# Banded attention and a gated MLP on one core: where the block transposes stand in TensorE's stream, and when the output additions run

## The chip, the cores and the metric

The kernel runs on one core of one Trainium2 chip. The metric is the device time of one execution in microseconds (us), as the median of several runs. The engines are TensorE (PE, with its weight loads shown as PEld), VectorE (DVE), ScalarE (ACT), GpSimd (POOL) and SyncE (SP, which issues the DMAs). Each works through its own queue in the order in which the program lists its instructions, and engines wait for one another through semaphores.

## The reference

Eight sequences of 576 positions, eight heads of 64. Half the heads attend to the last 32 positions, the other half to every fourth of the last 128. The attention output goes through an RMS norm and a gated MLP.

```python
scores = scale * np.matmul(q, k.transpose(0, 1, 3, 2))
mask_plain = (rel >= 0) & (rel < window)                                   # window 32
mask_dil = (rel >= 0) & (rel < window * dilation) & (rel % dilation == 0)  # dilation 4
...
attn = np.exp(scores)
attn = attn / (np.sum(attn, axis=-1, keepdims=True) + 1e-09)
return np.matmul(attn, v).astype(np.float32)
...
xn = x / rms * rms_g                       # x: 4608 tokens x 512
g = xn @ w_gate                            # 512 x 1536
silu = g * (1.0 / (1.0 + np.exp(-g)))
val = xn @ w_val
return (silu * val @ w_out).astype(np.float32)
```

## The kernel before

**Units and ticks.** The 4608 tokens are cut into 16 units of 288 (half a sequence). For a unit u, attention produces x, transposed (512 features on partitions in four chunks of 128, 288 tokens free), and the MLP consumes it. The MLP runs over NJ = 12 slices of the hidden size. Each slice is three *ticks*: a gate group (`gate`), a val group (`val`) and the projection of the slice before (`proj`). A tick is 12 large matmuls of 128x128 by 288, since every product is made of three fp32r matmuls (high by high, high by low, low by high; L637, L638, L639 in `three`). Behind the group of a tick `attend` puts the attention work that the plan has for that tick; it belongs to the next unit.

**Blocks.** The attention of a unit is 14 *blocks*: for each of the four chunks (two heads each) three blocks of 96 queries (chunks 0 and 1, plain window) or four of 72 (chunks 2 and 3, dilated). A block goes through these steps:
- scores (`scored`, L499): one matmul per head into a PSUM tile "s"
- maxima (`scores_max`): DVE adds the mask (L370) and finds the row maxima (L375); then ACT exponentials (`scores_exp`, L386), DVE sums and reciprocals (`scores_norm`, L395 and L396), and POOL's scaling (L402)
- transposes (`transposed`, L474): two fp32 transposes on PE, one per head, into a free part of the PSUM tile that the tick's gate or val group wrote, or into a tile of its own on a projection tick
- copies of the transposed block (`untranspose`): ACT makes the high part `pt` (L457), DVE the low part (L459)
- outputs (`output`): two matmuls, L487 with both parts and L488, into a PSUM tile "o", of which there is one
- `take`: ACT copies one part of "o" out (L422); `add`: DVE adds the other part to it (L432), two instructions each

Beside this, for each pair of heads, queries and keys are split into high and low parts (`split`): ACT copies, POOL makes the low part of the keys (L344), DVE that of the queries (L353). Of the MLP, ACT does tanh (L676), DVE the silu part (L681) and the product (L694), ACT and POOL the high and low part of the product (L705, L706).

**The order.** `plan` gives each block a tick for its scores (`q_at`), its transposes (`t_at`) and its outputs (`o_at`), relative to a base of the unit. For units 3 to 15 scores come every second tick from -9 to 17, transposes 5 ticks and outputs 8 ticks behind them. So scores and outputs share a tick, with an even one between that has transposes alone. Work of the other engines is queued by `later(dt, rank, fn)`: it is issued dt ticks on, ahead of that tick's group, in the order of ranks. The ranks that matter here, in the tick of issue: sums of `scores_norm` -1, tanh and product 0, `untranspose` 0.2, `take` and the product's parts 0.5, `scores_max` 0.7, silu part 0.8, queries' low part 0.9, exponentials 2, `add` 4. Positions of a relative tick modulo three tell the group: 0 gate, 1 val, 2 projection. Units below NEX = 3 have blocks in plain fp32 and no additions, and units 1 and 2 have lists of their own (`SCORES`).

Of the kernel before, what the change touches and what calls it, by code (L numbers as in the profile page):

```python
# [29 lines left out]
NEX = 3  # L30
# [28 lines left out]
def geometry(u, c):  # L59


    half = u % 2
    if c < NC // 2:
        if half:
            return [(QB * i, QB * i, 0, P) for i in range(U // QB)], QB, U + W
        return [(QB * i, max(QB * i - W, 0), 0 if i else W, P if i else QB)
                for i in range(U // QB)], QB, U
    nq = U // DIL
    keys = nq + (W if half else 0)
    return [(nq * r, keys * r, 0 if half else W, keys) for r in range(DIL)], nq, keys * DIL  # L70
# [3 lines left out]
def attn_moe(ctx: ExitStack, tc: tile.TileContext, qk_in, v_in, w_gate, w_val, w_out, rms_g, outT):  # L74
# [41 lines left out]
    def later(dt, rank, fn):  # L116
        put_off.setdefault(now[0] + dt, []).append((rank, fn))
# [168 lines left out]
    def load_v(b):  # L286

        if b is not None and b[0] >= NNAT:
            u, c, i = b
            vt = sb.tile([P, 2, D], F32, tag="vt", name=f"vt_{u}_{c}_{i}", bufs=3)  # L290
            nc.sync.dma_start(out=vt.rearrange("p a d -> p (a d)"), in_=v_in[u, c][:, i * 2 * D:(i + 1) * 2 * D])
            vs[b] = vt

    def further(b, n):

        k = everything.index(b) + n
        return everything[k] if k < len(everything) else None
# [6 lines left out]
    def split_v(b, dt):  # L304
        k = everything.index(b) % 2

        def hi():
            if k not in vparts:
                vparts[k] = [late[0].tile([P, 2, D], F32R, name=f"v{p}_{k}", bufs=1) for p in ("hi", "lo")]
            A.copy(out=vparts[k][0], in_=vs[b])  # L310

        def lo():
            vh, vl = vparts[k]
            G.tensor_tensor(out=vl, in0=vs.pop(b), in1=vh, op=ALU.subtract)  # L314
            load_v(further(b, 3))

        later(dt, 3.3, hi)
        later(dt, 5.1, lo)

    def after(u, h, n):  # L320

        k = u * H + h + n
        return divmod(k, H) if k < NU * H else None
# [82 lines left out]
    def take(u, c, i, o):  # L406

        blocks, nq, _ = geometry(u, c)
        if (u, c) not in xraw:
            xraw[u, c] = sb.tile([P, U], F32, tag="xraw", name=f"xraw_{u}_{c}", bufs=NC)  # L410
        x = xraw[u, c]
        if c < NC // 2:
            to = x[:, QB * i:QB * i + nq]
        else:
            to = x.rearrange("p (j r) -> p r j", r=DIL)[:, i, :]
        copy = V.tensor_copy if i % 2 and u == 0 and c == NC - 1 else A.copy
        if u < NEX:
            for a in range(2):
                copy(out=to[a * D:(a + 1) * D], in_=o[a * D:(a + 1) * D, a * nq:(a + 1) * nq])
        else:  # L420
            for a in range(2):
                A.copy(out=to[a * D:(a + 1) * D], in_=o[a * D:(a + 1) * D, (2 + a) * nq:(3 + a) * nq])  # L422
        if i == len(blocks) - 1:
            later(1, 2.5 if u else 1.9, lambda: square(u, c))

    def add(u, c, i, o):
        _, nq, _ = geometry(u, c)
        x = xraw[u, c]
        to = x[:, QB * i:QB * i + nq] if c < NC // 2 else x.rearrange("p (j r) -> p r j", r=DIL)[:, i, :]
        for a in range(2):  # L430
            rows = slice(a * D, (a + 1) * D)
            V.tensor_tensor(out=to[rows], in0=o[rows, a * nq:(a + 1) * nq], in1=to[rows], op=ALU.add)  # L432
# [18 lines left out]
    def untranspose(b, t_ps):  # L451
        blocks, nq, _ = geometry(*b[:2])
        n = blocks[b[2]][3]
        t_in = t_ps[:n].rearrange("k (a q) -> k a q", a=2)[:, :, :nq]
        exact = b[0] < NEX
        st[b] = pt = sb.tile([P, 2, 2, QB], F32 if exact else F32R, tag="pt", name=f"pt_{b[0]}_{b[1]}_{b[2]}", bufs=2)
        A.copy(out=pt[:n, 0, :, :nq], in_=t_in)  # L457
        if not exact:
            V.tensor_tensor(out=pt[:n, 1, :, :nq], in0=t_in, in1=pt[:n, 0, :, :nq], op=ALU.subtract)  # L459

    def products(q, t, o, t_ps, s_tag="s", o_tag="o"):


        if q:
            s_ps = ps.tile([P, 512], F32, tag=s_tag, name=f"s_{q[0]}_{q[1]}_{q[2]}")
        if o:
            o_ps = ps.tile([P, 512], F32, tag=o_tag, name=f"o_{o[0]}_{o[1]}_{o[2]}")
            pt = st.pop(o)
        if t:
            p, _ = st.pop(t)  # L470
        def transposed(a):
            blocks, nq, _ = geometry(*t[:2])
            n = blocks[t[2]][3]
            PE.transpose(t_ps[:n, a * QB:a * QB + nq], p[:nq, a, :n], ident[:nq, :nq])  # L474

        def output(a):
            blocks, nq, _ = geometry(*o[:2])
            n = blocks[o[2]][3]
            if a:
                return  # L480
            out = o_ps[:, :2 * nq].rearrange("d (a q) -> d a q", a=2)
            if o[0] < NEX:
                PE.matmul(out, vs.pop(o)[:n].rearrange("k a d -> k (a d)"), pt[:n, 0, :, :nq], start=True, stop=True)
                return
            vh, vl = (part[:n].rearrange("k a d -> k (a d)") for part in vparts[everything.index(o) % 2])
            both = o_ps[:, :4 * nq].rearrange("d (t a q) -> d t a q", t=2, a=2)
            PE.matmul(both, vh, pt[:n, :, :, :nq], start=True, stop=False)  # L487
            PE.matmul(out, vl, pt[:n, 0, :, :nq], start=False, stop=True)  # L488

        def scored(a):  # L490
            blocks, nq, _ = geometry(*q[:2])
            qc, kc, _, n = blocks[q[2]]
            sv = s_ps[:QB].rearrange("q (a t k) -> q a t k", a=2, t=2)
            if q[0] < NEX:
                qk = heads[q[0], 2 * q[1] + a]
                PE.matmul(sv[:nq, a, 0, :n], qk[:, qc:qc + nq], qk[:, U + kc:U + kc + n], start=True, stop=True)
                return
            qs, ks = heads[q[0], 2 * q[1] + a]
            PE.matmul(sv[:nq, a, :, :n], qs[:, qc:qc + nq], ks[:, :, kc:kc + n], start=True, stop=True)  # L499

        parts = [(b, fn, a) for b, fn in ((t, transposed), (o, output), (q, scored)) for a in range(2)]
        for b, fn, a in parts:
            if b:
                fn(a)
        if t:
            later(1, 0.2, lambda: untranspose(t, t_ps))
        if o:
            later(1, 0.5, lambda: take(*o, o_ps))
            if o[0] >= NEX:
                later(1, 4, lambda: add(*o, o_ps))  # L510
            if o[0] < NEX:
                later(1, 9, lambda: load_v(further(o, 3)))
            far = further(o, 2)
            if far and far[0] >= NEX:
                split_v(far, 8 if o[0] < NEX else 1)
        if q:
            later(1, 0.7, lambda: scores_max(*q, s_ps))
            later(2, 2, lambda: scores_exp(*q))
            later(3 if q[0] < NNAT else 4, -1, lambda: scores_norm(*q))
            u, c, i = q  # L520
            nxt = after(u, 2 * c, 2)
            nb = len(geometry(u, c)[0])
            if u < NEX:
                if u == NNAT - 1 and c == NC - 1 and i == nb - 1:
                    for h in range(4):
                        later(1, 9, lambda h=h: load(NNAT, h))
                if u >= NNAT and i == nb - 1 and c < NC - 1:
                    for a in range(2):
                        later(1, 9, lambda a=a: load(*after(u, 2 * c + a, 4)))
                if u == NEX - 1 and c == NC - 1 and i == nb - 1:  # L530
                    for a in range(2):
                        later(3 + a, 9, lambda a=a: split(NEX, a, (1, 2, 2, 3), G, V))
            elif nxt and i == 0:
                split(*nxt, (1, 2, 2, 3), G, V)
                split(nxt[0], nxt[1] + 1, (2, 3, 3, 4), G, V)
# [242 lines left out]
    plan(0, 0, range(nb), range(LAG, nb + LAG), range(LAG + OUT, nb + LAG + OUT))  # L778
    for u in range(1, NU):
        q_at = [LAST - (LAST - EARLY) * (nb - 1 - k) // (nb - 1) for k in range(nb)]  # L780
        t_at, o_at = [t + 5 for t in q_at], [t + 8 for t in q_at]
        if u <= NNAT:
            q_at = SCORES[u]
            t_at, o_at = [t + 5 for t in q_at], [t + (7 if u < NNAT else 8) for t in q_at]
        plan(u, ends - 2 + 3 * NJ * (u - 1), q_at, t_at, o_at)
# [20 lines left out]
    for u in range(NU):  # L806
        for j in range(NJ):
            for part in range(0 if u + j else 2, 3):
                t = 3 * (u * NJ + j) + part
# [94 lines left out]
```

## Time and profile before

| | |
|---|---|
| median of 3 runs | 1129.47 us (1128.94 to 1130.58) |
| profiled execution | 1129.25 us, its span 1127.4 us |
| granted TensorE clock | 1.000 |
| PE busy | 1116.9 us, 99% of the span |
| DVE, ACT, POOL busy | 779.8 us (69%), 700.6 us (62%), 602.5 us (53%) |
| chain that ended last | PE 94%, DVE 2%, DMA, issue, POOL and ACT 1% each |

The span is the time from the first to the last instruction in one profiled execution. In a timeline row the columns are start, duration, engine, line, operation, output and inputs, shapes, and how many instructions were merged ("x2"); in brackets the idle time before, with what ended it. A matmul's duration contains its way through the array, and matmuls overlap, so distances between starts tell what one costs. In a grouped row the number behind the bar is the busy time in us, then the mean duration in ns. In a row of the waits stand the waiting engine with tile and line, what released it, the total in us, the number of waits and the longest.

### The profile page before, as it was taken

To read this page: it belongs to the slowest core of one execution; us is meant where nothing else is said; L and a number is where in the kernel's file an instruction comes from. 1 tells how busy PE (TensorE), PEld (TensorE's weight loads), DVE (VectorE), ACT (ScalarE), POOL (GpSimd) and SP (SyncE) were. 2 spreads that over 40 slices of the span, in tenths; PEclk is the share of its full clock that TensorE was granted. 3 is DMA by queue.
4 is the path that set the end of the run, shared out by engine and by line. 5 is a ranking of instruction groups with operands and counts; after the bars stand their busy time and mean duration, and the time that the engine had idled before them with its cause. 6 is when DMAs were issued, how large, how long until landed. Compare 5 with 4: busy or idle time off the path is not lost.

```text
span 1127.4 us, 25853 instructions
## 1 busy us (share of the span) xinstructions
PE 1116.9 (99%) x8385; PEld 1088.4 (97%) x8385; DVE 779.8 (69%) x2837; ACT 700.6 (62%) x2578; POOL 602.5 (53%) x1051
## 2 busy tenths in 40 slices
PE   9999999999999999999999999999999999999998
PEld 7787999999999999999999999999999999999998
DVE  6888768758587675867758587675868767586311
ACT  6795576757667575666757576575756757575311
POOL 8323566646556554655646565564655646475211
PEclk9999999999999999999999999999999999999999
DMA  9566212303122121311212122131312212120000
GB/s 252 172 223 220 71 43 68 100 26 90 40 81 61 31 82 40 93 52 50 85 39 83 41 71 65 34 89 36 96 44 65 76 34 82 41 81 15 10 14 22
DMA packets 61544, 82.19 MB, mean 73 GB/s; under 512 B 7298, under 2 KB 41090, under 8 KB 61410
## 3 DMA queue, kind: packets, MB, share of 16 engines
q1 hardware_dynamic: 61410, 80.54, 23.6%
q8 instruction: 67, 1.10, 0.4%
q14 instruction: 67, 0.55, 0.2%
HBM read 71.08 MB, written 9.44 MB: 71 GB/s over the span
## 4 chain that ended last, share of the span: by engine, by line
PE 94%; DVE 2%; DMA 1%; issue 1%; POOL 1%; ACT 1%; SPq 0%; POOLq 0%; DVEq 0%; ACTq 0%
PE acc L637 9%; PE v L637 9%; PE g L637 9%; PE acc L638 8%; PE acc L639 8%; PE g L638 8%; PE v L638 8%; PE v L639 8%; PE g L639 8%; PE s L499 3%; PE o L487 3%; PE acc L634 2%; PE v L634 2%; PE g L634 2%; PE o L488 1%; PE t L474 1%
## 5 line engine op out<-in xcount | busy, mean ns | idle before, releaser
L706 POOL TENSOR_TENSOR hlo<-th,hhi 128x288 fp32r<-128x288 f32 x180 | 146.0, 811 | 202.3 <-ACT hhi L705 151.9
L639 PE MATMUL acc<-hhi,lo 128*128 128x288 f32 x720 | 212.4, 295 | 0.0
L402 POOL TENSOR_SCALAR t<-t,sum 72x72 f32<-72x72 f32 (+3 forms) x414 | 153.5, 383 | 73.9 <-DVE sum L396 63.8
L639 PE MATMUL g<-xhi,lo 128*128 128x288 f32 x612 | 180.2, 295 | 0.0
L639 PE MATMUL v<-xhi,lo 128*128 128x288 f32 x612 | 180.2, 294 | 0.0
L705 ACT CAST hhi<-th 128x288 fp32r<-128x288 f32 x180 | 78.1, 434 | 153.0 <-DVE th L694 150.4
L386 ACT ACTIVATE t<-t,sum 96x128 f32<-96x128 f32 (+3 forms) x448 | 166.0, 375 | 10.8 <-DVE sum L375 10.3
L676 ACT ACTIVATE th<-g 128x288 f32<-128x288 f32 x180 | 73.8, 410 | 107.2 <-PE g L639 89.2
L314 POOL TENSOR_TENSOR vlo<-vt,vhi 128x128 fp32r<-128x128 f32 x182 | 86.2, 473 | 101.3 <-ACT vhi L310 87.4
L639 PEld LDWEIGHTS acc<-hhi,lo 128*128 128x128 f32 x720 | 135.4, 188 | 0.0
L432 DVE TENSOR_TENSOR xraw<-o,xraw 64x72 f32<-64x72 f32 (+1 forms) x364 | 99.2, 273 | 50.5 <-ACT xraw L422 44.6
L681 DVE SCALAR_TENSOR_TENSOR th<-th,g 128x288 f32<-128x288 f32 x180 | 80.5, 447 | 71.3 <-ACT th L676 67.5
L639 PEld LDWEIGHTS g<-xhi,lo 128*128 128x128 f32 x612 | 115.2, 188 | 0.0
L639 PEld LDWEIGHTS v<-xhi,lo 128*128 128x128 f32 x612 | 115.1, 188 | 0.0
L637 PE MATMUL g<-xhi,hi_g 128*128 128x288 f32 x357 | 111.4, 312 | 0.8 <-DVE th L694 0.8
L637 PE MATMUL acc<-hhi,hi_o 128*128 128x288 f32 x360 | 110.7, 307 | 0.0
L694 DVE TENSOR_TENSOR th<-th,v 128x288 f32<-128x288 f32 x180 | 81.5, 453 | 38.0 <-PE v L639 30.0
L638 PE MATMUL acc<-hlo,hi_o 128*128 128x288 f32 x360 | 106.4, 296 | 0.0
L422 ACT COPY xraw<-o 64x72 f32<-64x72 f32 (+1 forms) x364 | 94.1, 258 | 11.7 <-PE o L488 9.6
L370 DVE TENSOR_TENSOR t<-s,mask 96x256 f32<-96x256 f32 (+3 forms) x182 | 66.8, 367 | 47.6 <-PE s L499 42.9
L344 POOL TENSOR_TENSOR ks<-qk,ks 128x288 fp32r<-128x288 f32 (+2 forms) x104 | 99.6, 973 | 0.0
L638 PE MATMUL g<-xlo,hi_g 128*128 128x288 f32 x322 | 94.9, 295 | 0.0
(189 smaller groups left out, 3566.5 us busy)
## 6 DMA issues: line engine op xcount, KB each, us to landing
qk<-in_qk_dram SPq DMA_DIRECT2D x60, 288.0 KB, 2.9
vt<-in_v_dram SPq DMA_DIRECT2D x196, 64.0 KB, 1.8
qk<-in_qk_dram SPq DMA_DIRECT2D x30, 352.0 KB, 3.0
out_dram<-ot SPq DMA_DIRECT2D x64, 144.0 KB, 1.9
qk<-in_qk_dram SPq DMA_DIRECT2D x30, 304.0 KB, 2.8
raw<-in_w_gate_dram SPq DMA_DIRECT2D x12, 512.0 KB, 4.5
raw<-in_w_val_dram SPq DMA_DIRECT2D x12, 512.0 KB, 5.3
raw<-in_w_out_dram SPq DMA_DIRECT2D x12, 512.0 KB, 4.5
```

Of the source, the lines that this page charges most:

```text
L314: G.tensor_tensor(out=vl, in0=vs.pop(b), in1=vh, op=ALU.subtract)
L344: ek.tensor_tensor(out=ks[:, 1, :nkt], in0=kr, in1=ks[:, 0, :nkt], op=ALU.subtract)
L386: A.activation(out=t[:nq, a, :n], in_=t[:nq, a, :n], func=AF.Exp, scale=-1.0, bias=sm[:nq, a, 0:1], accum_out=sm[:nq, a, 1:2] if u or i % ...
L402: (V if u == 0 and (c, i) > (NC - 1, 0) else G).tensor_scalar(out=t[:nq, a, :n], in0=t[:nq, a, :n], scalar1=sm[:nq, a, 3:4], scalar2=1.0, ...
L422: A.copy(out=to[a * D:(a + 1) * D], in_=o[a * D:(a + 1) * D, (2 + a) * nq:(3 + a) * nq])
L432: V.tensor_tensor(out=to[rows], in0=o[rows, a * nq:(a + 1) * nq], in1=to[rows], op=ALU.add)
L637: PE.matmul(out, wh[:, cc, :], xh, start=start, stop=False)
L638: PE.matmul(out, wh[:, cc, :], xl, start=False, stop=False)
L639: PE.matmul(out, wl[:, cc, :], xh, start=False, stop=stop)
L681: V.scalar_tensor_tensor(out=t, in0=t, scalar=1.0, in1=g, op0=ALU.add, op1=ALU.mult)
L694: V.tensor_tensor(out=t, in0=t, in1=v_ps[:, :U], op=ALU.mult)
L706: G.tensor_tensor(out=lo, in0=t, in1=hi, op=ALU.subtract)
```

## The change

For units 3 to 15 the transposes move from 5 to 6 ticks behind their block's scores, so that they fall on the tick that has outputs and scores of other blocks; outputs stay at 8. Within such a tick the order becomes outputs, transposes, scores in place of transposes, outputs, scores. Ticks without transposes, or with transposes of units 0 to 2, are issued in the old order. The additions move from the tick behind the outputs (rank 4, near its end) to the tick after that (rank 0.3, behind sums and product).

```diff
-        parts = [(b, fn, a) for b, fn in ((t, transposed), (o, output), (q, scored)) for a in range(2)]
+        order = ((o, output), (t, transposed), (q, scored))
+        if not t or t[0] < NEX:
+            order = ((t, transposed), (o, output), (q, scored))
+        parts = [(b, fn, a) for b, fn in order for a in range(2)]
...
             if o[0] >= NEX:
-                later(1, 4, lambda: add(*o, o_ps))
+                later(2, 0.3, lambda: add(*o, o_ps))
...
         q_at = [LAST - (LAST - EARLY) * (nb - 1 - k) // (nb - 1) for k in range(nb)]
-        t_at, o_at = [t + 5 for t in q_at], [t + 8 for t in q_at]
+        t_at, o_at = [t + 6 for t in q_at], [t + 8 for t in q_at]
```

## The prediction

> **What bounds the kernel now.** I read the page's busy shares first, then the waits, then TensorE's timeline by the start of each instruction, then the timelines of VectorE (DVE) and ScalarE (ACT) around one block.
>
> ```profile
> PE 1116.9 (99%) x8385; PEld 1088.4 (97%) x8385; DVE 779.8 (69%) x2837; ACT 700.6 (62%) x2578; POOL 602.5 (53%) x1051
> PE o L487 <- DVE xraw L432: 0.3, 1, 0.3
> ACT pt L457 <- DVE th L694: 91.5, 65, 1.9
> ```
>
> TensorE is busy all through and almost never waits: the wait view has 0.3 us for the output matmul L487 behind an addition. So time can be won only by a denser PE stream, and any new wait of PE is paid in full. DVE at 69% has no bound of its own, but its queue is in order. The third row: ACT's copy of the transposed block waits until DVE's product has read the same PSUM tile.
>
> The price of a transpose pair, standing alone between two groups (96 wide, then 72 wide):
>
> ```profile
> 605.44 0.33 PE L474 MATMUL v<-ident,t 96*128 96x96 f32 x2
> 605.55 0.38 PE L637 MATMUL acc<-hhi,hi_o 128*128 128x288 f32 x1
> 605.77 0.29 PE L638 MATMUL acc<-hlo,hi_o 128*128 128x288 f32 x1
> ...
> 706.11 0.29 PE L474 MATMUL v<-ident,t 72*72 72x72 f32 x2
> ...
> 706.42 0.29 PE L638 MATMUL acc<-hlo,hi_g 128*128 128x288 f32 x1
> ```
>
> ```profile
> L474 PE MATMUL g<-ident,t 96*128 96x96 f32 x62 | 10.2, 246 | 0.0
> L474 PE MATMUL v<-ident,t 72*104 72x72 f32 x42 | 6.1, 225 | 0.0
> L637 PEld LDWEIGHTS acc<-hhi,hi_o 128*128 128x128 f32 x360 | 67.7, 188 | 0.0
> L499 PEld LDWEIGHTS s<-ks,qs 128*72 128x72 f32 x208 | 22.9, 142 | 0.0
> ```
>
> ```profile
> 614.90 0.34 PE L487 MATMUL o<-pt,vhi 128*128 128x384 f32 x1
> 615.07 0.25 PE L488 MATMUL o<-pt,vlo 128*128 128x192 f32 x1
> 615.16 0.36 PE L499 MATMUL s<-ks,qs 128*72 128x208 f32 x2
> 615.35 0.31 PE L637 MATMUL v<-xhi,hi_g 128*128 128x288 f32 x1
> ...
> 618.72 0.29 PE L487 MATMUL o<-pt,vhi 104*128 104x288 f32 x1
> ...
> 708.00 0.23 PE L488 MATMUL o<-pt,vlo 72*128 72x144 f32 x1
> 708.07 0.34 PE L637 MATMUL g<-xhi,hi_g 128*128 128x288 f32 x1
> 708.25 0.29 PE L638 MATMUL g<-xlo,hi_g 128*128 128x288 f32 x1
> ```
>
> From 615.35 to 618.72 lie 24 large matmuls and one transpose pair. With the pair at 0.18 (next sentence) a large matmul takes (3.37 - 0.18) / 24 = 0.133 us. From the first transpose to the second large matmul pass 0.33 us (96 wide) or 0.31 (72); less one large matmul, a pair costs 0.197 or 0.177. Its inside: two merged transposes take 0.33, one 0.246, so the second starts 0.084 after the first; at 72, 0.29 - 0.225 = 0.065. That leaves 0.112 from the second transpose to the large matmul, for either width. The short output matmul L488 shows the same: 708.00 to 708.25 is 0.25, less 0.133, so 0.117 in rounded rows. So a short matmul ahead of a large one costs 0.11, whatever it streams; I read that as the 128 weight columns of the large one, loaded while nothing long covers them. The score matmul's load is shorter, 142 against 188 ns: 0.112 - 0.046 = 0.066.
>
> **The change, part by part.** It concerns units 3 to 15, 13 units of 14 blocks; units 0 to 2 keep the order, the ticks of the transposes and have no additions.
>
> *Transposes between outputs and scores.* Now the pair stands alone in the tick between two block ticks; then it follows the output matmuls and precedes the scores of other blocks, or the next group where no scores come. The step into the pair is covered in both places (the short output matmul streams 0.07 to 0.09 anyway, and had the score weights to cover). The step out of it falls from 0.112 to the transposes' own pace, 0.084 or 0.065, since 0.066 of score weights fit in. Saved: 0.028, say 0.026 at 96, and 0.045 at 72. Where no scores follow, the 0.112 behind L488 goes and L488's own 0.066 stays: 0.045 too. Bounds: nothing, if the scores' load after a transpose is as dear as a large one's; 0.112 per block, if the step out vanished.
>
> ```profile
> L432 DVE TENSOR_TENSOR xraw<-o,xraw 64x72 f32<-64x72 f32 x208 | 59.6, 286 | 46.4 <-ACT xraw L422 43.2
> L432 DVE TENSOR_TENSOR xraw<-o,xraw 64x96 f32<-64x96 f32 x156 | 39.6, 254 | 4.1 <-ACT xraw L422 1.4
> ```
>
> Two additions a block make 104 blocks of 72 and 78 of 96: 104 x 0.045 + 78 x 0.026 = 6.7 us saved. The Trainium skill ("TensorE: Matmul & The Clock Gate", section on LDWEIGHTS) has a weight load take its columns divided by 1.2 ns, so 107 ns for 128 columns and 60 for 72; by it the saving would be 22 and 42 ns a block, 6.1 us. The trace agrees: 188 - 142 = 46 ns for 56 columns.
>
> *One tick more between scores and transposes, one less between transposes and outputs.* GpSimd's normalisation gets a tick more, and nothing waited for it. ACT's copy and DVE's low part (L457, L459) lose one of three ticks. No DMA is issued by a moved step, and SP's and GpSimd's queues keep their order. But the copy and the low part (rank 0.2) now stand in the tick after a block tick, ahead of the maxima of its scores (rank 0.7), and DVE cannot start the maxima before them.
>
> *Additions one tick later, rank 0.3.* They leave the end of that tick and go behind the next tick's sums (rank -1) and product (rank 0). There is one PSUM tile "o": the next outputs wait for the addition, and outputs now lead the block's PE work, so transposes and scores queue behind that wait. Before, they had slack:
>
> ```profile
> 615.62 0.37 DVE L370 TENSOR_TENSOR t<-s,mask 72x208 f32<-72x208 f32 x1 [0.84 <-PE s L499]
> 616.41 0.45 DVE L681 SCALAR_TENSOR_TENSOR th<-th,g 128x288 f32<-128x288 f32 x1
> 616.77 0.52 DVE L432 TENSOR_TENSOR xraw<-o,xraw 64x96 f32<-64x96 f32 x2
> 617.32 0.15 DVE L395 TENSOR_REDUCE sum<-sum 72x2 f32<-72x4 f32 x1
> 617.71 0.45 DVE L694 TENSOR_TENSOR th<-th,v 128x288 f32<-128x288 f32 x1
> ```
>
> ```profile
> 620.73 0.29 PE L474 MATMUL g<-ident,t 72*104 72x72 f32 x2
> 621.11 0.41 ACT L676 ACTIVATE th<-g 128x288 f32<-128x288 f32 x1
> 621.42 0.27 ACT L457 CAST pt<-g 104x144 fp32r<-104x144 f32 x1
> 621.72 0.31 DVE L459 TENSOR_TENSOR pt<-g,pt 104x144 fp32r<-104x144 f32 x1 [0.37 <-ACT pt L457]
> 621.95 0.44 DVE L681 SCALAR_TENSOR_TENSOR th<-th,g 128x288 f32<-128x288 f32 x1
> 682.60 0.30 DVE L370 TENSOR_TENSOR t<-s,mask 72x144 f32<-72x144 f32 x1 [0.83 <-PE s L499]
> 683.25 0.45 DVE L681 SCALAR_TENSOR_TENSOR th<-th,g 128x288 f32<-128x288 f32 x1
> ```
>
> ```profile
> 730.69 0.41 DVE L370 TENSOR_TENSOR t<-s,mask 96x256 f32<-96x256 f32 x1
> 731.67 1.40 DVE L353 TENSOR_TENSOR qs<-qk,qs 64x288 fp32r<-64x288 f32 x1
> 733.10 0.52 DVE L432 TENSOR_TENSOR xraw<-o,xraw 64x96 f32<-64x96 f32 x2
> ...
> 733.77 0.41 PE L487 MATMUL o<-pt,vhi 128*128 128x384 f32 x1
> 734.02 0.25 PE L488 MATMUL o<-pt,vlo 128*128 128x192 f32 x1
> 690.79 1.01 DVE L353 TENSOR_TENSOR qs<-qk,qs 64x288 fp32r<-64x288 f32 x1
> ```
>
> I work in time after the first large matmul behind a block's scores; the next outputs are due 24 x 0.133 = 3.2 us later. The pair stands 0.26 before that zero (scores start 0.19 before it, 615.16 to 615.35, and a 72-wide transpose 0.065 earlier) and ends at -0.03.
>
> *Gate ticks* (a block tick behind a gate group: relative ticks 3, 9 and 15 of a unit, taking positions modulo three from the code). ACT's tanh reads the transposes' PSUM tile, so it starts 0.09 behind their end (621.02 to 621.11), copy 0.31 and low part 0.61 after tanh's start: the low part at 0.67, the maxima 0.23 later (621.72 to 621.95) at 0.90. Maxima 0.79 (615.62 to 616.41): the silu part at 1.69. Then 0.36 (616.41 to 616.77), sums and reciprocal 0.39 (617.32 to 617.71), the product 0.38 (0.45 long, overlapped like the silu part): the addition at 2.82, ending at 3.34 (0.52), or 3.40 at 72 (two of 0.286). PE starts 0.15 after that (733.62 to 733.77) and its first output matmul holds 0.25 instead of 0.17 (615.07 - 614.90): 0.22 in all, so 3.56 to 3.62 against 3.2. With 0.05 for a wider low part at tick 3, the wait is about 0.4 in the 7 odd units. In the 6 even units the maxima of 72 keys take 0.65 (682.60 to 683.25): 0.26. Together 21 x 0.40 + 18 x 0.26 = 13 us.
>
> *Val and projection ticks.* Behind a val group the product comes first (0.45), then copy and low part: maxima at about 1.07, no silu or second product before the addition; it ends at 2.8 to 2.9, in time by 0.1 to 0.2. Behind a projection the copy goes at once, and the addition ends near 2.4.
>
> *Where a query's low part (L353) stands between maxima and addition* (ticks -1, 5 and 13): beside GpSimd's key parts it takes 1.40, 0.84 to 1.03 or, undisturbed, 0.46. Tick 13 (val): 1.07 + 0.79 + 1.0 + 0.39 + 0.59 + 0.22 = 4.06, 0.85 late; with 0.84, 0.7. Tick -1: 0.45 late in even units; 1.0 in odd ones (1.40), where the trace already has about 0.25 (o1 at 733.77). Tick 5: 0.34 in even units, none in odd. That is 7 x 1.45 + 6 x 1.6 = 20 us; with 0.46 throughout it is 3. GpSimd's work shifts too, so I cannot place the overlap; I take 15, nearer to the rows shown.
>
> **The sum.** The profiled execution took 1129.25 us (span 1127.4 and 1.85 around it; the median, 1129.47, is the same within 0.02%). 1129.25 - 6.7 + 13 + 15 = 1150.5 us, 1.9% more.
>
> **The rivals.**
> A. *The denser stream alone; the additions land in time.* One mechanism: the chain from the transposes to the addition is 0.4 us shorter than I add up, as when DVE's overlaps are larger or the maxima go earlier. The additions decide from 3.2 us on: under 2.98 at their end costs nothing. For it: DVE is idle 31% of the time, and val and projection ticks have room. Against it: each interval in the chain is a measured row, and the order is fixed by ranks. Time: 1129.25 - 6.7 = 1122.5, or 1121 with the old waits of tick -1 gone (7 x 0.25).
> B. *Only the gate ticks wait, the query parts run undisturbed.* For it: odd units had 0.46 at tick 5. Against: overlap elsewhere. 1129.25 - 6.7 + 13 + 3 = 1138.5.
> C. *The pair does not become cheaper*: the scores' weights after an f32 transpose load as slowly as a large matmul's, and with the additions in time nothing changes: 1129, 1130. Against it: the load's length follows its columns.
> D. *The waits are larger*: with the query parts at their full length and 0.2 more at each of 39 gate ticks from ACT's queue (copy behind late exponentials), 1129.25 - 6.7 + 13 + 20 + 8 = 1163.5.
>
> **How the numbers follow.** A difference under about 0.2% (2.3 us) is what a measurement here can't tell from none. Forecast 0.37, B 0.2, D 0.1: slower, 0.67. A 0.25: faster. C 0.08: same. The likeliest case is the forecast, 1150.5, with 1141 (q parts between B and mine) to 1157 (all of the 20) as its own range. The range over all goes from A's 1121 to 1159, leaving out D's upper part and the lowest tail.
>
> **What would show it.** In the changed profile the gap between a transpose pair's end and the scores should be 0.065 to 0.084 us instead of 0.112 to a large matmul; PE's waits should show L487 released by DVE's L432 some 50 to 80 times, 15 to 30 us in total, at gate ticks and at ticks -1, 5, 13. DVE's low part should come ahead of the maxima, and DVE idle before it behind ACT's copy. If L487 has no such waits and the time is near 1122, the chain was shorter than summed (A); if PE has the waits and the pair still costs 0.18, C's half is right. Most likely to make me wrong: the overlap of L353 with GpSimd, and a DVE interval of 0.2 us that overlaps in the new order.

## The result and the profile after

The changed kernel takes 1160.29 us (median of 5 runs, 1158.71 to 1160.75) against 1129.0 us before: a ratio of 1.027, 95% interval 1.0259 to 1.0281. The span of the profiled execution went from 1127.4 to 1158.5 us. Predicted were 1150.5 us and a range from 1121 to 1159: slower, as forecast, but by 31.3 us instead of 21, and just outside the range.

The page of the changed kernel: busy times, and the chain that ended last (before, PE had 94% of it).

```profile
PE 1129.6 (98%) x8385; PEld 1084.9 (94%) x8385; DVE 743.9 (64%) x2837; ACT 701.2 (61%) x2578; POOL 598.5 (52%) x1051
PE 77%; DVE 11%; ACT 7%; issue 2%; DMA 2%; POOL 1%; POOLq 0%; SPq 0%; ACTq 0%; DVEq 0%
```

DVE does less than before (743.9 us busy against 779.8) and yet stands in the chain. The waits of the changed kernel say why (waiting engine, tile and line; releaser; total us, count, longest us; behind line 501 the lines of the changed kernel are 3 higher):

```profile
DVE pt L459 <- ACT pt L457: 182.2, 175, 3.0
PE o L487 <- DVE xraw L432: 12.0, 26, 0.6
PE v L640 <- DVE pt L459: 5.9, 12, 0.8
PEld v L640 <- DVE pt L459: 11.4, 23, 1.0
PEld o L487 <- ACT t L386: 17.3, 26, 0.8
PEld o L487 <- ACT hhi L708: 4.6, 21, 0.4
```

The row of L459 in the kernel before:

```profile
DVE pt L459 <- ACT pt L457: 39.6, 97, 0.8
```

PE has two new waits. The first was forecast: the output matmul L487 behind the addition. The second was not: the val group L640 behind DVE's low part L459, which reads the PSUM tile that this group takes next (the expectations call its place a bank). And DVE stands idle 182 us, not 40, for ACT's copy of the transposed block.

The view counts only idle time and splits a wait between PE and its weight loads (PEld). The last two rows are no other cause: the records have all 63 weight loads of outputs before which PEld stood idle for over 0.15 us start 0.115 to 0.117 us after the end of an addition (26 + 21 named ACT, 16 without a name). So I also take, from the records of the 182 blocks, the distance from the start of each L487 (and of the L488 behind it) to the instruction ahead, less its undisturbed pace, and the same for large matmuls within groups: **outputs wait 29.5 us (2.9 before), groups 12.7 (none before)**. The starts say what each waits for: 72 of the 182 output matmuls wait, and each starts 0.145 to 0.148 us after the end of an addition; 26 val groups wait, and each starts 0.055 us after the end of a low part. With the forecast 6.7 for the denser stream, 1127.4 - 6.7 + 26.6 + 12.7 = 1160.0 against the measured span of 1158.5. In all kernels below that have the new order this account comes out 1.5 to 2.4 us above the span.

One block behind a projection (tick -1 of an odd unit) shows both. ACT's timeline of the changed kernel:

```profile
609.08 0.43 ACT L708 CAST hhi<-th 128x288 fp32r<-128x288 f32 x1 [1.50 <-DVE th L697]
609.42 0.43 ACT L620 CAST spare<-xraw 128x288 fp32r<-128x288 f32 x1
609.76 0.40 ACT L386 ACTIVATE t<-t,sum 96x128 f32<-96x128 f32 x1
...
610.54 0.52 ACT L339 CAST ks<-qk 128x416 fp32r<-128x416 f32 x1
610.97 0.43 ACT L348 CAST qs<-qk 128x288 fp32r<-128x288 f32 x1
611.30 0.30 ACT L457 CAST pt<-t 128x192 fp32r<-128x192 f32 x1
```

DVE's:

```profile
608.62 0.43 DVE L697 TENSOR_TENSOR th<-th,v 128x288 f32<-128x288 f32 x1
609.88 0.91 DVE L621 TENSOR_TENSOR xlo<-xraw,spare 128x288 fp32r<-128x288 f32 x1 [0.83 <-ACT spare L620]
611.64 0.36 DVE L459 TENSOR_TENSOR pt<-t,pt 128x192 fp32r<-128x192 f32 x1 [0.85 <-ACT pt L457]
611.91 0.41 DVE L370 TENSOR_TENSOR t<-s,mask 96x256 f32<-96x256 f32 x1
...
612.90 0.60 DVE L353 TENSOR_TENSOR qs<-qk,qs 64x288 fp32r<-64x288 f32 x1
...
613.80 0.50 DVE L432 TENSOR_TENSOR xraw<-o,xraw 64x96 f32<-64x96 f32 x2
```

PE's:

```profile
609.27 0.34 PE L487 MATMUL o<-pt,vhi 128*128 128x384 f32 x1
...
609.94 0.29 PE L640 MATMUL g<-xhi,hi_g 128*128 128x288 f32 x1
...
611.39 0.29 PE L642 MATMUL g<-spare,lo 128*128 128x288 f32 x1
612.05 0.40 PE L640 MATMUL v<-xhi,hi_g 128*128 128x288 f32 x1 [0.37 <-DVE pt L459]
...
614.46 0.41 PE L487 MATMUL o<-pt,vhi 128*128 128x384 f32 x1 [0.55 <-DVE xraw L432]
```

The block's outputs start at 609.27, and its transposes and scores are through by 610.1. But ACT comes to the copy only at 611.30: the product's high part, another cast, exponentials and copies of keys and queries stand ahead in its queue. DVE meanwhile has the maxima to do, whose scores are there, and stands in order for the copy. The low part ends at 612.00; the val group starts at 612.05 instead of 611.52. Maxima, query part, sums and addition take 2.30 us from there (612.00 to 614.30), but PE has only the twelve matmuls of that group, 1.6 us, before the next outputs: these wait too, 0.79 us on average by the account.

### The profile page after: what moved, and what is told of

Read it like the earlier page. It is cut to its first block, busy times and chain, and to the rows that moved or that the text cites. A ratio compares the mean times of both kernels' runs of the same rounds, so it can differ in the third digit from the quotient of the medians.

```text
span 1158.5 us, 25708 instructions
## 1 busy us (share of the span) xinstructions
PE 1129.6 (98%) x8385; PEld 1084.9 (94%) x8385; DVE 743.9 (64%) x2837; ACT 701.2 (61%) x2578; POOL 598.5 (52%) x1051
## 4 chain that ended last, share of the span: by engine, by line
PE 77%; DVE 11%; ACT 7%; issue 2%; DMA 2%; POOL 1%; POOLq 0%; SPq 0%; ACTq 0%; DVEq 0%
PE acc L640 7%; PE g L640 7%; PE acc L641 7%; PE g L641 7%; PE g L642 7%; PE acc L642 7%; PE v L640 6%; PE v L642 6%; PE v L641 6%; PE o L487 3%; PE s L499 2%; DVE t L375 2%; PE acc L637 2%; PE v L637 2%; ACT t L386 2%
## 5 line engine op out<-in xcount | busy, mean ns | idle before, releaser
L402 POOL TENSOR_SCALAR t<-t,sum 72x72 f32<-72x72 f32 (+3 forms) x414 | 151.0, 377 | 67.3 <-DVE sum L396 59.8
L642 PE MATMUL g<-xhi,lo 128*128 128x288 f32 x612 | 180.2, 294 | 0.0
L432 DVE TENSOR_TENSOR xraw<-o,xraw 64x72 f32<-64x72 f32 (+1 forms) x364 | 97.2, 267 | 20.5 <-ACT xraw L422 18.0
L640 PE MATMUL acc<-hhi,hi_o 128*128 128x288 f32 x360 | 108.9, 302 | 0.0
L640 PE MATMUL g<-xhi,hi_g 128*128 128x288 f32 x357 | 107.6, 301 | 0.8 <-DVE th L697 0.8
L344 POOL TENSOR_TENSOR ks<-qk,ks 128x288 fp32r<-128x288 f32 (+2 forms) x104 | 97.5, 952 | 0.0
L375 DVE CUSTOM_DVE_ANT_0 t<-s,t 96x128 f32<-96x128 f32 (+3 forms) x364 | 81.5, 259 | 6.3
```

Source lines behind the costliest of these rows:

```text
L344: ek.tensor_tensor(out=ks[:, 1, :nkt], in0=kr, in1=ks[:, 0, :nkt], op=ALU.subtract)
L375: V.tensor_tensor_reduce(out=t[:nq, a, :n], in0=sv[:nq, a, 0, :n], in1=plus, op0=ALU.add, op1=ALU.min, scale=-(0.5 if u == NNAT else 1.0) ...
L402: (V if u == 0 and (c, i) > (NC - 1, 0) else G).tensor_scalar(out=t[:nq, a, :n], in0=t[:nq, a, :n], scalar1=sm[:nq, a, 3:4], scalar2=1.0, ...
L640: PE.matmul(out, wh[:, cc, :], xh, start=start, stop=False)
L642: PE.matmul(out, wl[:, cc, :], xh, start=False, stop=stop)
```

## The experiments

Two explanations were tried first. **The additions' new place** costs the waits (then undoing it, or doing it alone, tells). Or **DVE's idleness in order**: the low part, at rank 0.2 ahead of ready work, makes DVE wait for ACT, and each delay comes back through product, high part and copy. The letters in the quoted expectations name the theories as they stood at each time; they are not the prediction's rivals. Intervals are 95%, of the ratio to the kernel before as it was timed beside each. The waits are those of one profiled execution, whose time can lie 1 to 2 us from the median.

| kernel | median us | ratio | outputs wait us | groups wait us | DVE waits for the copy us |
|---|---|---|---|---|---|
| before | 1129.0 | 1 | 2.9 | 0 | 39.6 |
| after | 1160.29 | 1.0259 to 1.0281 | 29.5 | 12.7 | 182.2 |
| 1 additions back | 1168.22 | 1.0329 to 1.036 | 11.9 | 39.1 | 186.6 |
| 2 additions alone | 1166.01 | 1.031 to 1.0341 | 39.4 | 0 | 94.2 |
| 3 additions back, old order | 1165.11 | 1.0301 to 1.0332 | 18.7 | 32.8 | 180.2 |
| 4 low part late | 1136.32 | 1.0045 to 1.0079 | 4.9 | 13.6 | 49.7 |
| 5 low part by group | 1133.64 | 1.0029 to 1.0059 | 5.6 | 12.6 | 69.1 |
| 7 low part late, additions back | 1144.84 | 1.0126 to 1.016 | 0.6 | 26.5 | 55.8 |
| 8 low part late, old order | 1139.21 | 1.0076 to 1.0106 | 14.1 | 14.3 | 49.3 |
| 11 additions alone, ahead | 1131.72 | 1.001 to 1.0028 | 5.2 | 0 | 30.4 |
| 14 ACT copies moved | 1151.58 | 1.019 to 1.0218 | 32.8 | 0.8 | 161.2 |
| 13 = 5 with ACT copies moved | 1132.33 | 1.0019 to 1.0043 | 8.1 | 5.5 | 63.3 |
| 15 = 13, low part early behind projections | 1139.83 | 1.0089 to 1.0116 | 20.5 | 1.8 | 120.1 |
| 17 = 13 with additions ahead of sums | 1130.86 | 1.001 to 1.0028 | 2.4 | 11.1 | 59.0 |

(In 3 and 8 the outputs' column holds a constant share of the old order, where L488 follows L487 later. The outputs that start right behind an addition's end wait 7.0 us there in 3 and 0.8 in 8.)

**1. Additions back** in their old place, the rest of the change as it is; **3** the same with the old order in the tick.

```diff
-                later(2, 0.3, lambda: add(*o, o_ps))
+                later(1, 4, lambda: add(*o, o_ps))
```

> The changed kernel with the additions put back to the tick behind the outputs (rank 4). Theory A (the late additions hold up the outputs): behind gate ticks the waits of the output matmuls go (8 us of 29.5), at ticks 1 and 7 they shrink by the 0.39 us of the sums, to about 8 us in all; the waits of val groups (12.7 us) stay, since they hang on the copy of the transposed block; about 1139 us. Rival B (the waits come from the transposes' new tick alone, the place of the additions does not matter): 1157 to 1160 us.

> As e1_add_back, but within a tick transposes come first again, then outputs, then scores. Theory A: the pair is followed by 128 weight columns again, so the 6.7 us of the denser stream are lost, while ACT and DVE start on the transposed block 0.26 us earlier, which takes up to 0.26 us from each of some 50 waits: between e1_add_back and 7 us above it. If the saving does not come from the order, it is equal to e1_add_back or below.

Both main figures missed. The outputs' waits fell by 17.6 us as they should, but the groups' rose by 26.4, and the whole got slower: the additions now stand ahead of the product, so the product's high part on ACT and the copy behind it come later (read from the order, not tried alone). The new place is not what makes the changed kernel slow; in this layout it is the better one. With the old order (3) the time fell by 3.1 us instead of rising, which is the expectation's other branch, that the order saves nothing. The account says otherwise: from 1 to 3 the outputs' waits fall by 4.9 us (11.9 to 7.0) and the groups' by 6.3, and of these 11.2 us the looser stream takes back 6.7. That leaves 4.5, and the two profiled spans differ by 4.4.

**2. The additions' new place alone**, on the kernel before; **11** the same at rank 0.1, ahead of the low part.

```diff
-                later(1, 4, lambda: add(*o, o_ps))
+                later(2, 0.3, lambda: add(*o, o_ps))   # 2;  11: later(2, 0.1, ...)
```

> The kernel before with nothing but the additions moved one tick on (rank 0.3). Theory A: with the maxima at the head of their tick the additions end at about 3.0 us of the 3.4 that they have, so only the odd units' first outputs wait longer, by 0.39 us: 1130 to 1135 us. Rival C (the additions' move alone makes most of the loss): 1145 us or more.

> The kernel before with the additions one tick on, but at rank 0.1: behind sums and product, ahead of the transposed block's low part (as e2_add_only, which has them at 0.3, behind it). Theory E (in e2_add_only the additions waited behind the low part, which waits for ACT's copy of a transpose issued only one tick earlier): nearly all of its 37 us go, 1130 to 1135 us. If sums and product alone make the additions late: 1150 us or more.

The wait of DVE for the copy in kernel 2:

```profile
DVE pt L459 <- ACT pt L457: 94.2, 144, 1.4
```

Its timelines in one tick, by engine:

```profile
622.56 0.33 PE L474 MATMUL v<-ident,t 96*128 96x96 f32 x2
...
623.42 0.32 ACT L457 CAST pt<-v 128x192 fp32r<-128x192 f32 x1 [1.13 <-DVE th L694]
...
623.77 0.36 DVE L459 TENSOR_TENSOR pt<-v,pt 128x192 fp32r<-128x192 f32 x1 [0.39 <-ACT pt L457]
624.04 0.51 DVE L432 TENSOR_TENSOR xraw<-o,xraw 64x96 f32<-64x96 f32 x2
...
624.71 0.42 PE L487 MATMUL o<-pt,vhi 128*128 128x384 f32 x1 [0.20 <-DVE xraw L432]
```

In the old layout copy and low part run in the tick in which the additions now fall. The additions need nothing fresh, but stand behind the low part, which does: 37 us. At rank 0.1 instead of 0.3, 34 of them are gone. The first was a miss, the second within its figure.

**4. The low part behind the maxima** (rank 0.75), else the changed kernel; **5** the same, but the low part early (0.25) behind val groups.

```diff
-        if not exact:
-            V.tensor_tensor(out=pt[:n, 1, :, :nq], in0=t_in, in1=pt[:n, 0, :, :nq], op=ALU.subtract)
...
+            if t[0] >= NEX:
+                later(1, 0.75, lambda: low_part(t, t_ps))
```

(`low_part` is the line taken out, as a function of its own.)

> The changed kernel with DVE's low part of the transposed block behind the maxima (rank 0.75 in place of 0.2). Theory A: DVE's chain starts 0.4 us earlier, so the waits of outputs behind gate ticks go (8 us); but the low part frees the PSUM tile 0.8 us later, so the groups that reuse its bank wait longer, by 20 to 30 us in all: 1170 to 1185 us. Rival B, and any theory in which DVE's order within the tick plays no part: 1160 us.

> e4_low_late with the low part back ahead of the maxima (rank 0.25) at val ticks alone, where the tile's bank is wanted 1.6 us later by the next gate group. Theory D (DVE idles in its order for ACT's copy; the low part must only be early where the bank is wanted soon): the waits of groups behind blocks at ticks 1, 7 and 13 go (5 us), the rest stays: 1130 to 1133 us. If the low part ahead of the maxima is dear at val ticks too: 1138 us or more.

Kernel 4's waits:

```profile
DVE pt L464 <- ACT pt L457: 49.7, 43, 2.1
DVE t L370 <- PE s L504: 102.5, 91, 2.0
```

One instruction a block moved behind the maxima of the same tick (L370 and two of L375), and 24.0 of the 31.3 us are gone. Both figures of the expectation missed, 1170 to 1185 us and 1160. DVE's wait for the copy falls from 182 to 50 us; what it waits for instead is scores that PE hasn't made yet, which costs PE nothing. This shows the main cause: not how much DVE has to do, but that it stood in order behind a copy that wasn't ready. The Trainium skill ("PSUM — Partial Sum Buffer", section on engine and sequencer instructions) calls the queues of ScalarE, VectorE and GpSimd strict FIFO; the 0.85 us ahead of L459 at 611.64, with ready maxima behind it, agree. Kernel 5 takes 2.7 us more off, close to its figure, though the two intervals overlap.

**7 and 8**: kernel 4 with the additions back at (1, 4), and kernel 4 with the old order.

> e4_low_late with the additions back in the tick behind the outputs (rank 4). Theory D: the waits of outputs (4.9 us) go, but the product and with it ACT's exponentials and the next copy come 0.5 us later, which adds 5 to 15 us of waits of val and gate groups: 1136 to 1147 us. Theory A as first written (late additions alone make the loss): 1131 us.

> e4_low_late with transposes ahead of outputs within a tick. The denser stream's 6.7 us are lost and some waits shrink as ACT starts 0.26 us earlier: 3 to 7 us above e4_low_late, so 1139 to 1143 us. If the order saves nothing: 1136 us or less.

Both as expected. 7: the new place of the additions is worth 8.5 us here, through the groups' waits (26.5 against 13.6). 8: the order outputs, transposes, scores is worth 2.9 us net.

**6, 9, 10 and 12: the query parts.** 6 and 9 are kernel 5 with the ticks of the splits changed, to get the query's low part away from maxima and additions; 10 is 9 with the low part late behind gate groups alone; 12 is the splits of 9 on the kernel before.

```diff
-                split(*nxt, (1, 2, 2, 3), G, V)
-                split(nxt[0], nxt[1] + 1, (2, 3, 3, 4), G, V)
+                split(*nxt, (1, 2, 1, 2), G, V)               # 6: (1, 2, 1, 3)
+                split(nxt[0], nxt[1] + 1, (3, 4, 3, 4), G, V) # 6: (3, 4, 3, 5)
```

> e5_val_early with ACT's copies of the next heads' keys and queries moved out of the odd ticks, where they stand ahead of the copy of the transposed block, into even ones, behind it. Theory D: the late copy behind ticks -1 and 5 comes early, and the waits of val groups there (8 us in e4_low_late) go: 1122 to 1126 us, under the kernel before. If those waits come from something else than ACT's order: as e5_val_early.

> e5_val_early with ACT's copies for the next heads in even ticks (as in e6_splits), but DVE's low parts of the queries in odd ticks, where they stand behind the additions. Theory D: the copies' gain of e6_splits (7 us fewer waits of val groups) stays and its waits of outputs behind ticks 1, 7 and 15 (14 us of 23) go: 1122 to 1127 us, below the kernel before. If the order of these splits does not carry the waits: 1133 us.

> e9_splits_odd with the low part ahead of the maxima at projection ticks too, so that only gate ticks have it behind. Theory D: ACT's copy is early there now, so DVE hardly idles for it and the val group two ticks later gets its bank 0.8 us sooner: 1 to 4 us below e9_splits_odd. If DVE's idling for the copy still counts: above it.

> The kernel before with the splits of e9_splits_odd and nothing else. Its stream has 2.9 us of waits of outputs to win, so 1126 to 1130 us; what e9_splits_odd is below this is due to the transposes' place and not to the splits.

6, 9 and 12 missed by 18 to 25 us: 1147.09 (1.0145 to 1.0175), 1145.30 (1.0118 to 1.0157) and 1151.28 us (1.0177 to 1.0208). The control 12 says that the new ticks themselves cost 22 us. In 6 the groups' waits fell from 12.6 to 5.8 as meant, but the outputs' rose to 23.5, since the second low part came between maxima and additions in other ticks. In 9 and 12 it meets GpSimd, and the groups wait (in 9 for 27.5 us, the outputs hardly at all); that the longer query part is what delays them is read from the order. Kernel 9, the timelines of DVE and of GpSimd:

```profile
602.39 1.24 DVE L353 TENSOR_TENSOR qs<-qk,qs 64x288 fp32r<-64x288 f32 x1
...
602.00 1.31 POOL L344 TENSOR_TENSOR ks<-qk,ks 128x416 fp32r<-128x416 f32 x1
```

The group of L353 by line (busy us, mean ns) in the kernel before:

```profile
L353 DVE TENSOR_TENSOR qs<-qk,qs 64x288 fp32r<-64x288 f32 x104 | 82.5, 793 | 9.3 <-ACT qs L348 6.5
```

and in kernel 12:

```profile
L353 DVE TENSOR_TENSOR qs<-qk,qs 64x288 fp32r<-64x288 f32 x104 | 108.1, 1040 | 3.2
```

That is 25.6 us more of DVE. The Trainium skill ("SBUF — State Buffer", section "Who interferes with whom") has a DVE instruction with two SBUF inputs contend with a GpSimd instruction that reads SBUF; L353 beside L344 agrees, with 1.24 us against 0.46 undisturbed. Kernel 10 (1142.65 us, 1.0102 to 1.0132) came 2.65 below 9, as expected.

**13 to 16: ACT's copies.** In the block shown, copies of keys and queries stand ahead of L457. How much is theirs? 14 is the changed kernel with two of them moved to other ticks, 13 the same on kernel 5, 15 is 13 with the low part late behind gate groups alone, 16 the kernel before with the moved copies.

```diff
+                split(*nxt, (1, 2, 1, 3), G, V)
+                split(nxt[0], nxt[1] + 1, (3, 3, 3, 4), G, V)
```

> The changed kernel with two of ACT's four copies for the next heads (0.43 and 0.54 us) moved from the odd tick, ahead of the copy of the transposed block, to the even ticks beside it, behind that copy; all low parts stay in their ticks. Theory D (the waits of val groups at ticks -1 and 5, which the sum of the prediction lacked, are ACT's copy standing behind these two): 12.7 us of such waits fall to 3 to 5, and the outputs at ticks 1 and 7 wait less by up to 0.5 us each: 1140 to 1148 us. Rival F (the copy is late because ACT waits for DVE's product, whatever else stands in its queue): 1157 to 1161 us.

> e5_val_early with the same two copies moved. Theory D: its 12.6 us of waits of val groups fall to 4 to 6: 1125 to 1129 us. Rival F: 1133 us.

> e13_copies with the low part ahead of the maxima at projection ticks too. If the copy is early there, the bank is free 0.8 us sooner: 1123 to 1127 us. If DVE still idles for it: above e13_copies.

> The kernel before with the same two copies moved and nothing else: 1128 to 1132 us, since it has no waits there to lose.

16 took 1128.46 us (0.9991 to 1.0009): by themselves the moved copies change nothing. In 14 they take away 8.7 us, between the two figures: the groups' waits are gone (0.8 of 12.7 us), but the outputs' rose, from 29.5 to 32.8. At tick -1 the low part and the maxima now come early, and the query part behind them meets GpSimd's key parts, so that it takes 1.15 us where the block shown above has 0.60. Kernel 14's timelines of DVE and of GpSimd:

```profile
606.98 1.15 DVE L353 TENSOR_TENSOR qs<-qk,qs 64x288 fp32r<-64x288 f32 x1
...
605.29 2.52 POOL L344 TENSOR_TENSOR ks<-qk,ks 128x416 fp32r<-128x416 f32 x2
```

and the group of L353, of the changed kernel, then of 14:

```profile
L353 DVE TENSOR_TENSOR qs<-qk,qs 64x288 fp32r<-64x288 f32 x104 | 71.2, 684 | 2.9
```

```profile
L353 DVE TENSOR_TENSOR qs<-qk,qs 64x288 fp32r<-64x288 f32 x104 | 82.4, 792 | 2.9
```

So the groups' wait was ACT's key and query copies ahead of L457. The outputs' wait has two causes, either of which is enough: maxima late behind the low part, or a long query part behind them. 13 is only 1.3 below 5, at the expectation's other figure, and the intervals overlap: its groups' waits fell as theory D has it, from 12.6 to 5.5, but the outputs' rose by 2.5, and the profiled execution of 5, from which its 12.6 comes, took 1.8 us more than its median. 15 is 7.5 above 13: behind projections, too, DVE must not stand and wait for the copy (120 us of waits against 63).

**17 and 18: the rest.** 13 with the additions ahead of the sums where no product comes, and (18) ahead of the product too.

```diff
-                later(2, 0.3, lambda: add(*o, o_ps))
+                later(2, 0.3 if (now[0] + 2) % 3 == 1 else -2, lambda: add(*o, o_ps))  # 18: -2 always
```

> The version of copies with the low parts behind the maxima (1132.3 us) keeps waits of the outputs of 8.1 us (0.54 and 0.11 at tick 1, 0.22 at tick 15) and of the val groups of 5.5. Here the additions go ahead of the sums (rank -2) in ticks without a product; behind a product they stay at 0.3. Theory D (the additions end just too late, and nothing else hangs on the sums): sums and reciprocal, 0.31 to 0.39, no longer stand ahead; tick 15 loses all of 0.22 x 13, tick 1 0.31 and 0.11: 5.7 us less, 1126.5 to 1128.5. Rival G: the sums are now late, GpSimd scales late, and the transposes or the key parts wait: 1132 or more.

> The same, but with the additions ahead of sums and product in the product's ticks too (ticks 5, 11 and 17, 39 blocks). Theory D says that whatever delays the product by 0.5 delays the product's high part on ScalarE, the copy behind it and the low part, and so the val groups: their waits rise from about 5 to 8 to 14 us, 1129 to 1136. Rival H (the product has slack there): the same time as the one beside it.

17 missed: 1130.86 us, 1.5 below 13 instead of 4 to 6. The outputs' waits went as expected, from 8.1 to 2.4 us, but the groups' came up from 5.5 to 11.1. The trace has 4.8 of these 5.6 us at the gate groups two ticks behind the val blocks of ticks 1 and 7, which don't wait in 13. Each of them starts 0.145 to 0.147 us after the end of a low part. DVE's timeline of kernel 17 behind tick 1 of an odd unit:

```profile
601.62 0.48 DVE L353 TENSOR_TENSOR qs<-qk,qs 64x288 fp32r<-64x288 f32 x1
602.13 0.45 DVE L704 TENSOR_TENSOR th<-th,v 128x288 f32<-128x288 f32 x1
602.97 0.36 DVE L464 TENSOR_TENSOR pt<-v,pt 128x192 fp32r<-128x192 f32 x1 [0.38 <-ACT pt L457]
```

The copy waits for the product, which stands behind a second query part and starts 0.52 us after the first large matmul behind the scores (601.61), in 13 at 0.11. The outputs ahead no longer wait, so PE is earlier, but DVE's work up to the product takes about as long, and the wait comes up at the group behind it instead. 18 took 1131.31 us (1.0015 to 1.0034), with the groups at 10.5 us: rival H, the product has slack there. On DVE, 18 has the additions where the kernel before has them, ahead of sums and product. That place cost 7.9 us in the changed kernel (1), 8.5 in 7, and nothing (1.0 less than in 13) here: a later product seems to be dear only while the copies of keys and queries and the low part's place leave it no slack; 18 differs from 7 in both, and no run parts them.

No version with moved transposes beats the kernel before; 17 comes nearest, at 1.0019 (1.001 to 1.0028).

## Why the prediction was right in sign and short in size

**The denser stream, -6.7 us: right.** PE's timeline of the changed kernel, a 96-wide pair with scores, and a 72-wide pair without:

```profile
618.38 0.34 PE L487 MATMUL o<-pt,vhi 128*128 128x384 f32 x1
...
618.64 0.33 PE L474 MATMUL g<-ident,t 96*128 96x96 f32 x2
...
619.00 0.31 PE L640 MATMUL v<-xhi,hi_v 128*128 128x288 f32 x1
...
720.28 0.29 PE L487 MATMUL o<-pt,vhi 72*128 72x288 f32 x1
...
720.49 0.29 PE L474 MATMUL v<-ident,t 72*72 72x72 f32 x2
...
720.79 0.29 PE L641 MATMUL acc<-hlo,hi_o 128*128 128x288 f32 x1
```

From L487 to the group's first matmul pass 0.62 us; before it was 0.45 (614.90 to 615.35) and 0.197 for the pair elsewhere: 0.027 saved, forecast 0.026. The 72-wide case takes 0.51 to the second large matmul, before 0.38 (707.87 to 708.25) and 0.177: 0.047, forecast 0.045. Rival C falls. Undoing the order in kernel 8 gave only 2.9 us back, and the records have the rest: outputs, due later there, wait 0.8 us in all instead of 4.9.

**The gate ticks, +13: right in kind, too large.** The chain ran as added up: the product at 621.40, the addition from 621.75 to 622.27, L487 at 622.41, where the forecast end was 3.34 us after 619.00, 622.34. Outputs at ticks 5, 11 and 17 wait 0.25 us in odd units (0.40 forecast) and 0.16 in even ones (0.26): 21 x 0.25 + 18 x 0.16 = 8.1 us. So this term of the sum was 5 us too large.

**The ticks with a query part, +15: 21 us, but mostly for another reason.** The outputs at ticks 1, 7 and 15 wait 13 x 0.79, 7 x 0.77 + 6 x 0.41 and 13 x 0.23 us. The last, behind the query part of tick 13, was forecast at 0.85 and 0.7; the second, behind tick 5, at none in odd units and 0.34 in even ones. In the block shown L353 takes 0.60, not 1.40: the addition is late because the maxima began at 611.91, behind a late copy. Over all units the query part takes 0.60 to 0.66 behind tick -1, 0.46 to 0.70 behind tick 5 and 0.46 to 0.53 in the place that counts behind tick 13. So its overlap with GpSimd's key parts, on which the prediction spent most of its doubt, did not occur in these places, and that 21 us lie near the 20 of "their full length" is luck.

**The step that failed is "Behind a projection the copy goes at once, and the addition ends near 2.4".** In the block shown the copy starts 1.36 us after the first large matmul behind the scores (609.94 to 611.30), not at once, and the addition ends 4.36 after it. The step held where no keys or queries are copied ahead: at ticks 11 and 17 the copy starts 0.0 to 0.4 us after that matmul, and the additions end at 2.1 to 2.5. At ticks -1 and 5 the copy starts at 1.0 to 1.3 and the additions end at 3.8 to 4.4, query part included. I had costed ACT only for tanh at gate ticks (rival D has 0.2 for it), and never asked when ACT would be free. And the step has a second price that the prediction didn't name: the low part is the last reader of a PSUM bank that the val group two ticks on takes. Ticks -1 and 5 lose 0.62 and 0.60 us in odd units there, 0.29 and 0.41 in even ones: 7 x 1.22 + 6 x 0.70 = 12.7 us. With the outputs at ticks 1 and 7 (10.3 and 7.9) 30.9 of the 42.2 us of waits hang on these blocks; in kernel 4, whose maxima don't wait for the low part, the outputs there wait 0.31 and 0.02 us in odd units instead of 0.79 and 0.77. The prediction had 15 us for these ticks and tick 13 together.

At tick 5 something is mixed in: in 5 of the 13 units the product's high part waits 1.7 us on average for an output's DMA, which holds the buffer that both use. ACT's waits for it in the changed kernel:

```profile
ACT hhi L708 <- DMA out_dram<-ot: 8.6, 5, 1.8
```

and in the kernel before:

```profile
ACT hhi L705 <- DMA out_dram<-ot: 1.1, 2, 0.9
```

In these five units the val group's first matmul waits 0.72 to 0.97 us there, in the other eight 0.06 to 0.21, so that this is worth some 3.4 us. With two copies moved (14) four units still have that wait:

```profile
ACT hhi L708 <- DMA out_dram<-ot: 5.3, 4, 1.5
```

There the groups hardly wait, but the outputs at tick 7 do, 1.30 to 1.31 us in the odd ones of these units against 0.82 to 0.85 in the other odd units. Nothing here tried the DMA alone.

The terms as measured: 1129.25 - 6.7 + 8.1 + 21.1 + 12.7 = 1164.4, less the 2.9 of old waits, which these contain, 1161.5; the profiled execution took 1160.29. Of the forecast signs, L487 released by additions 50 to 80 times for 15 to 30 us came true (72 times, 29.5 us). So did "DVE idle before it behind ACT's copy", but its size, 182 us, the prediction did not estimate, and the wait of the val groups was not among the signs.

**The rivals.** A falls, since the additions land late. The condition of B, query parts nearly undisturbed, came close to the truth, and yet its 1138.5 us is 22 short, since it too lacks the late copy. D is nearest with 1163.5, by luck: the query parts weren't long, and the gate ticks cost less than forecast, not more. (The prediction's own range ends at 1157 "with all of the 20"; its sum gives 1155.6 there.)

**Open:** how the outputs' waits at ticks 1 and 7 would divide between the late copy and the query part (14 takes away the first and brings in the second), and what the output's DMA would cost if nothing else were late.

## What to carry to other kernels

In an engine that works in order, place an instruction by when its inputs are ready, not by when its result is wanted: put one that waits for another engine's fresh output behind work that is ready, and if its result has a deadline (a PSUM bank that the next group takes counts as one), bring the producer forward instead. When a step is moved, walk the queue of every engine that serves it, also the one that seems to have room: DVE was 64% busy here, and the order of its work cost 24 us. A stream saving of 30 to 50 ns a block is gone with one wait of a quarter of a microsecond in every seven blocks.

## What the hardware showed that I had not expected

DVE's query part of 64x288 takes 0.46 us alone. Beside GpSimd's key parts it took 1.40 in the kernel before, 1.24 in kernel 9 and 1.15 in kernel 14, and shifts by one tick cost 25.6 us of DVE time in kernel 12. An overlap by itself does not make it long: behind tick 5 of an odd unit of the kernel before it takes 0.46 (from 609.28) while the key parts run from 608.26 to 610.69. From the end of an addition to the output matmul that waited for it lay 0.145 to 0.148 us in all 72 cases of the changed kernel and all 105 of kernel 2.
